# Half of the gate tiles through Gelu straight from PSUM, and a new order of all engines, in a two-layer attention and feed-forward kernel

## The chip, the cores and the metric

The kernel runs on one core of one Trainium2 chip. A core has five engines that run side by side, each through its own queue in order: TensorE (matrix products, PE in the profile), VectorE (DVE), ScalarE (ACT), GpSimd (POOL) and SyncE (SP, which here only issues DMA transfers). TensorE writes into PSUM, and VectorE and ScalarE read from there. The metric is the device time of one execution in microseconds (us).

## The reference

Two blocks A and B are applied in turn, A, B, A, B, to x of 2048 x 512 in bfloat16. A is attention with a compressive memory, over 4 segments of 512 rows, with 32 heads of 16; B is a gated feed-forward layer of inner width 1792.

```python
def A(x, wq, wk, wv, wo, beta):              # x is already layer-normed
    q, k, v = heads(x @ wq), heads(x @ wk), heads(x @ wv)      # 32 heads, 4 segments of 512
    phi = lambda t: where(t > 0, t + 1.0, exp(t))
    g = sigmoid(beta)
    M, z = 0, 0
    for s in range(4):
        p = softmax(q[s] @ k[s].T * 16 ** -0.5 + causal_mask)
        a_dot = p @ v[s]
        a_mem = (phi(q[s]) @ M) / (phi(q[s]) @ z + 1e-6)
        out[s] = g * a_mem + (1 - g) * a_dot
        M += phi(k[s]).T @ v[s];  z += phi(k[s]).sum(0)
    return out @ wo

def B(x, w_gate, w_up, w_down):
    return gelu_tanh(x @ w_gate) * (x @ w_up) @ w_down

x = x + A(layernorm(x));  x = x + B(layernorm(x))      # and both once more
```

## The kernel before, in words

The work falls into eight pieces, numbered k = 0 to 7: segment k % 4 of the first pass (k below 4) or of the second. Each piece has an attention part (class `Att`) and a feed-forward part (class `Ffn`), 512 rows each. Activations, x and all weights stay in SBUF. Almost all matrix products go through `product`, which issues four matmuls of 32 columns each, side by side on the array (profile line L392).

**Scores and exponentials.** A piece has 20 score steps, five for each group of eight heads. A step fills two PSUM tiles `st0` and `st1` (two banks each) by small matmuls (L786); ScalarE takes the exponential of each from PSUM to SBUF (L815, 128x1024, 320 in all); GpSimd clears what the causal mask hides (L806). After two or three steps a "flush" multiplies the result with v (L834). Since there is one `st0` and one `st1`, a score has to wait for the exponential that reads the same tile.

**Everything else** is an item: q, k and v products (`qk`, `v`), memory products (`mem`, `upd`), the output product `wo`, `gate`, `up`, `down`, and for three of the norms a transpose on TensorE (`turn`; the other transposes are DMAs, L357). Every item takes one of four PSUM banks `m0` to `m3`, until VectorE or ScalarE has read it out. `evict` posts such a copy to both engines, and the one that is free first takes it (L383 on VectorE, L384 on ScalarE).

**The order is planned when the program is built.** A small model (`Clocks`, `Engine`) keeps a clock for each engine with fixed costs, and emits the instructions in the order in which the model would run them. On the chip each queue then runs in that fixed order, and waits where the data is not there. At each turn the planner issues a score step if its PSUM tile is free; else the ready item with the lowest due date (`Item.due`, for example `k + 0.61` for `wo`, `k + 1.2` for `gate`); and if there is no ready item, a dummy product on the tile `warm`, whose result nobody reads:

```python
            if streams:
                ps = Psum()
                ...
                product(ps()[:], warm[:], wide)
```

ScalarE's and VectorE's jobs are served by ready time plus a slack (`EXP_SLACK`, `GELU_SLACK`, ...), the lowest first.

**Gelu.** ScalarE needs one function table for the exponentials and another for Gelu; a job with the other table puts a load ahead of it. Each `Ffn` has 14 gate tiles. For k = 0 to 6 they are copied from PSUM to the tile `gel`; when all 14 are there, `gelu_all` posts Gelu over `gel` in place, in groups of `GELU_TILES = 4` tiles (L986: three of 128x2048 and one of 128x1024), with no exponential between. For k = 7 each tile goes from PSUM through Gelu directly (L927), since no exponentials are left. VectorE multiplies `gel` by the up product (L953), then come the four down products.

Of the kernel before, what the change touches and what calls it, by code (L numbers as in the profile page):

```python
# [38 lines left out]
M_BANKS = 4  # L39
PT_STEPS = 5  # L40
SETS = 3
GELU_TILES = 4
QK_DUE = 0.75
E_Q = 0.0
E_K = 0.9

FLUSH_WAIT = 4.0
PIECE_SLACK = 2.0
URGENT, SOON, NORMAL = -4.0, -1.5, 0.0
EXP_SLACK, E_SLACK, PHI_SLACK, GELU_SLACK = -1.0, 3.0, 3.0, -1.0  # L50
ACT_EVICT, FIRST_EVICT = 0.5, 1.0
XN_BUFS = 3
KB_DVE = 1
KB_SLACK = 4.0
HALF_STEPS = 1
MARGIN = 1.0
MEM_SLACK = 1.0


class Engine:  # L60
# [2 lines left out]
    LATENCY = 0.055  # L63

    def __init__(self, overlap=0.0):
        self.free, self.overlap, self.jobs, self.table = 0.0, overlap, [], "exp"

    def post(self, ready, slack, *steps, table=None, taken=None):

# [14 lines left out]
    def serve(self, now):  # L84

        self.jobs = [j for j in self.jobs if not j[4]]
        if not self.jobs:
            return False
        start = max(self.free, min(j[0] for j in self.jobs) + self.LATENCY)
        if start > now:  # L90
            return False
        job = min((j for j in self.jobs if j[0] + self.LATENCY <= start + 0.03), key=lambda j: j[0] + j[1])
        ready, _, steps, table, taken = job
        taken.append(1)
        self.jobs.remove(job)
        t = ready
        if table and table != self.table:
            self.free += 1.28
            self.table = table
        for cost, emit, told in steps:  # L100
            t = max(self.free, t + self.LATENCY) + cost
            self.free = t - self.overlap
            if emit:
                emit()
            if told:
                told(t)
        return True


class Clocks:  # L110


    MM = {512: 0.2158, 128: 0.056}
    SMALL = 0.025
    SWITCH = 0.097

    def __init__(self):
# [100 lines left out]
def kernel(  # L218
# [278 lines left out]
    class Att:  # L497
        def __init__(self, k):
            self.k, self.s, self.tt0 = k, k % NSEG, TPS * (k % NSEG)
            self.norm = Norm(("xnTa", k), self.tt0, f"xnTa{k % 2}", NORMAL, lambda: k < 2 or ("qkv", k - 2) in ev)  # L500
# [9 lines left out]
        def add_items(self):  # L510
            k, s = self.k, self.s

            def storage():
                return k < SETS or (("scores", k - SETS) in ev and self.phi_done(k - SETS))
# [8 lines left out]
            def qk(b, w, done):  # L523
                ps = Psum()
                pairs = [(lambda kt=kt: w[:, kt, b * P:(b + 1) * P], lambda kt=kt: self.norm.xnT[:, kt, :])
                         for kt in range(KT)]
                return Item(k - QK_DUE + 0.01 * b, lambda: storage() and ck.has(("xnTa", k)), dense(ps, pairs),
                            lambda: (made(), self.counted(), done(b, ps)), kind="qk", ps=ps)

            def q_done(b, ps):  # L530
# [28 lines left out]
            def v(j):  # L559
                ps = Psum()  # L560
                pairs = [(lambda kt=kt: self.norm.xnT[:, kt, j * P:(j + 1) * P], lambda kt=kt: w_att["v"][:, kt, :])
                         for kt in range(KT)]

                def done():
                    self.counted()
                    evict(ps, lambda: by_head(self.vaug)[:, j, :, 0:DH],
                          lambda: ps()[:].rearrange("p (h e) -> p h e", e=DH),
                          lambda t: ev.update({("v", k, j): t}))

                return Item(k - QK_DUE + 0.04 + 0.01 * j if k else -0.61,  # L570
                            lambda: ck.has(("xnTa", k)) and (k < SETS or ("flush", k - SETS, 3, 1) in ev),
                            dense(ps, pairs), done, kind="v", ps=ps)

# [50 lines left out]
        def mem_items(self):  # L624
# [10 lines left out]
            def den_done():  # L635
                def add():
# [7 lines left out]
            items.append(Item(k + 0.01, lambda: ready() and (self.s == 1 or ("am", k - 1) in ev),  # L644
                              [(Clocks.SMALL, lambda j=j, b=b: den_mm(j, b)) for j in range(TPS) for b in range(4)],
                              den_done, kind="mem", ps=den))

# [43 lines left out]
        def upd_item(self):  # L691
# [13 lines left out]
            def done():  # L705
# [23 lines left out]
                else:  # L729
# [162 lines left out]
    class Ffn:  # L892
        def __init__(self, k):
            self.k, self.tt0, self.last = k, TPS * (k % NSEG), k >= NSEG
            self.norm = Norm(("xnTf", k), self.tt0, "xnTf", URGENT, lambda: k == 0 or ("up", k - 1) in ev)
            self.n_wo, self.n_gate, self.n_kept, self.n_up, self.n_down = 0, 0, 0, 0, 0

            def add_to_x(j, ps, slack, told):
                xt = x_sb[:, self.tt0 + j, :]
# [3 lines left out]
            def wo(j):  # L903
                ps = Psum()
                pairs = [(lambda kt=kt: att[k].aT[:, kt, j * P:(j + 1) * P], lambda kt=kt: w_att["o"][:, kt, :])
                         for kt in range(KT)]

                def done():
                    add_to_x(j, ps, URGENT, lambda t: self.norm.stats(j, t))
                    self.n_wo += 1  # L910
                    if self.n_wo == TPS:
                        ev["wo", k] = ck.pe

                return Item(k + 0.61 + 0.001 * j, lambda: ck.has(*[("aT", k, b) for b in range(4)]),
                            dense(ps, pairs), done, kind="wo", ps=ps)

            def gate(ft):
                ps = Psum()
                pairs = [(lambda kt=kt: wg_sb[:, kt, ft * P:(ft + 1) * P], lambda kt=kt: self.norm.xnT[:, kt, :])
                         for kt in range(KT)]  # L920

                def done():
# [3 lines left out]
                    if k == NK - 1:  # L926
                        ck.act.post(ck.made(), URGENT, (0.602, lambda: nc.scalar.activation(  # L927
                            out=self.gel[:, ft, :], in_=ps()[:], func=ACT.Gelu_apprx_tanh),
                            lambda t: (ps.read(t), ev.update({("gel", k, ft): t}))), table="gelu")
                        return  # L930

                    def told(t):
                        self.n_kept += 1
                        if self.n_kept == FT:
                            self.gelu_all(t)

                    evict(ps, lambda: self.gel[:, ft, :], lambda: ps()[:], told)

                return Item(k + 1.2 + 0.005 * ft,
                            lambda: ck.has(("xnTf", k)) and (k == 0 or ("down", k - 1) in ev),  # L940
                            dense(ps, pairs), done, kind="gate", ps=ps)

            def up(ft):
# [4 lines left out]
                def done():  # L948
                    self.n_up += 1
                    if self.n_up == FT:  # L950
# [6 lines left out]
                return Item(k + 1.3 + 0.02 * ft, lambda: ck.has(("gel", k, ft), by=ck.pe + 0.6), dense(ps, pairs), done,  # L957
                            kind="up", ps=ps)

            def down(j):  # L960
# [22 lines left out]
        def gelu_all(self, ready):  # L983
            def gelu(f0, f1):
                g = self.gel[:, f0:f1, :]
                return (0.205 + 0.427 * (f1 - f0), lambda: nc.scalar.activation(out=g, in_=g, func=ACT.Gelu_apprx_tanh),  # L986
                        lambda t: ev.update({("gel", self.k, ft): t for ft in range(f0, f1)}))

            ck.act.post(ready, GELU_SLACK, *[gelu(f, min(f + GELU_TILES, FT)) for f in range(0, FT, GELU_TILES)],
                        table="gelu")  # L990

    mem_state = {}
    st_free = [0.0, 0.0]
# [64 lines left out]
    def norm_of_input(s, at, gap):  # L1058
        for j in range(TPS):
# [1 line left out]

    norm_of_input(1, 11.7, 0.5)
    norm_of_input(2, 22.0, 1.0)
    ck.when(lambda: ("v", 1, 3) in ev and all(("k", 1, b) in ev for b in range(4)),
            lambda: norm_of_input(3, ck.pe, 2.0))


    streams = [(k, t) for k in range(NK) for t in range(STEPS)]
# [15 lines left out]
    def score_now(idle=False):  # L1084
        if not streams or not (step_free or half):
            return ()
        k, t = streams[0]
        if not att[k].score_ready(t):
            return ()
        free = [f <= ck.pe - 0.05 for f in st_free]  # L1090
        if half:
            return (1,) if free[1] else ()
        if all(free):
            return (0, 1)
        other = any(not j[4] and j[0] <= st_free[1] for j in ck.act.jobs)
        return (0,) if free[0] and (idle or k < HALF_STEPS and not other) else ()

    def open_item(got):
        it = min(got, key=lambda it: it.due)
# [86 lines left out]
```

## Time and profile before

| | |
|---|---|
| time, median of 3 runs | 565.4 us (564.77 to 566.05) |
| time of the profiled execution | 564.99 us |
| its span, first to last instruction | 563.2 us |
| TensorE matmul busy | 553.9 us (98%) |
| VectorE busy | 464.7 us (83%) |
| ScalarE busy | 446.8 us (79%) |
| GpSimd busy | 273.1 us (48%) |
| granted TensorE clock | 1.000 |

The span is what the trace shows; the time is 1.8 us longer. A group of instructions is a line, an engine, an operation, the tiles out<-in, the shape, xcount, then the busy time and the mean length of one in ns, then the idle time of the engine just before them and what ended it. Neighbouring instructions of an engine overlap a little, so a busy time can be below the count times the mean.

### The profile page before, as it was taken

What the parts mean: (1) busy time and instruction counts of PE and PEld (TensorE: products, weight loads), DVE (VectorE), ACT (ScalarE), POOL (GpSimd) and SP (SyncE); (2) the same over time, 40 slices, a digit from 0 to 9 for tenths busy, and PEclk for the clock granted to TensorE, in tenths of its full rate; (3) what the DMA queues carried; (4) which work ended last, traced back from release to release, by engine and by line L of the source; (5) the groups of instructions that cost most, each with busy time, mean ns of one, the idle gap of its engine ahead of it and who ended that gap; (6) DMA issues with size and microseconds to landing.
All of it is one profiled execution on the core that took longest, in us unless ns stands there. A gap on an engine that the chain in (4) does not pass through costs nothing.

```text
span 563.2 us, 24630 instructions
## 1 busy us (share of the span) xinstructions
PE 553.9 (98%) x10998; PEld 259.7 (46%) x10998; DVE 464.7 (83%) x881; ACT 446.8 (79%) x510; POOL 273.1 (48%) x520
## 2 busy tenths in 40 slices
PE   8999999999999999999999999999999999999997
PEld 4433445444445444444445444444444444445554
DVE  5977999999988899888978999889789976778061
ACT  3899999987899879997889878988799778970600
POOL 2589865465542459336553456535654354410000
PEclk9999999999999999999999999999999999999999
DMA  7236812801130016100210224002320004100001
GB/s 224 40 96 201 148 12 41 171 3 30 32 59 3 12 26 92 31 2 2 43 38 3 31 49 70 10 4 34 77 45 3 3 21 78 21 2 30 12 3 40
DMA packets 64362, 25.98 MB, mean 46 GB/s; under 512 B 54272, under 2 KB 64256, under 8 KB 64256
## 3 DMA queue, kind: packets, MB, share of 16 engines
q1 hardware_dynamic: 64112, 24.40, 21.4%
q8 instruction: 86, 1.41, 1.1%
q14 instruction: 20, 0.16, 0.1%
q10 hardware_dynamic: 144, 0.01, 0.0%
HBM read 9.71 MB, written 2.10 MB: 21 GB/s over the span
## 4 chain that ended last, share of the span: by engine, by line
PE 82%; DVE 15%; issue 1%; DMA 1%; POOL 0%; ACT 0%; DVEq 0%
PE m L392 66%; PE st L786 8%; PE m L834 5%; DVE st L415 2%; DVE x_sb L900 2%; DVE byq L846 1%; PE m L297 1%; DVE e L604 1%; DVE phiq L604 1%; DVE e L618 1%; DVE xn L445 1%; DVE aT L861 1%; DVE gel L383 1%; DMA amT<-am 1%; DVE ab L854 1%
## 5 line engine op out<-in xcount | busy, mean ns | idle before, releaser
L815 ACT ACTIVATE pt<-st 128x1024 bf16<-128x1024 f32 x320 | 310.4, 1027 | 56.4 <-PE st L786 52.6
L806 POOL TENSOR_SCALAR_AFFINE_SELECT pt<-pt 128x256 bf16<-128x256 bf16 (+1 forms) x448 | 205.6, 478 | 203.9 <-ACT pt L815 197.6
L392 PE MATMUL m<-xnT,wg_sb 128*32 128x512 bf16 x1792 | 107.9, 380 | 1.3 <-ACT xnT L384 0.7
L392 PE MATMUL m<-wd_sb,gel 128*32 128x512 bf16 x1792 | 105.3, 380 | 0.1
L392 PE MATMUL m<-xnT,wu_sb 128*32 128x512 bf16 x1792 | 104.1, 379 | 0.0
L953 DVE TENSOR_TENSOR gel<-gel,m 128x512 bf16<-128x512 bf16 x112 | 75.1, 684 | 26.9 <-PE m L392 25.5
L392 PEld LDWEIGHTS <-wu_sb 128*32 128x32 bf16 x1792 | 46.8, 97 | 46.6 <-issue 4.4
L392 PEld LDWEIGHTS <-gel 128*32 128x32 bf16 x1792 | 46.0, 97 | 46.0 <-issue 6.2
L392 PEld LDWEIGHTS <-wg_sb 128*32 128x32 bf16 x1792 | 45.5, 96 | 46.0 <-issue 10.3
L900 DVE TENSOR_TENSOR x_sb<-x_sb,m 128x512 bf16<-128x512 bf16 x64 | 42.5, 675 | 22.0 <-PE m L392 21.6
L846 DVE STREAM_TRANSPOSE byq<-m 128x512 f32<-128x512 f32 x64 | 45.0, 705 | 11.9 <-PE m L834 11.8
L543 POOL TENSOR_SCALAR kB<-kf,maskB 128x512 bf16<-128x512 bf16 x28 | 45.0, 1609 | 18.9 <-DVE kf L383 13.0
L383 DVE CAST gel<-m 128x512 bf16<-128x512 f32 x56 | 37.9, 683 | 10.7 <-PE m L392 10.3
L834 PE MATMUL m<-pt,vaug 128*32 128x512 bf16 (+3 forms) x1024 | 46.2, 300 | 0.1
L986 ACT ACTIVATE gel<-gel 128x2048 bf16<-128x2048 bf16 (+1 forms) x28 | 45.2, 1685 | 0.1
L415 DVE BATCH_NORM_STATS2 st<-x_sb 128x6 f32<-128x512 bf16 x60 | 40.6, 676 | 0.3
L786 PE MATMUL st<-q,kB 32*128 32x128 bf16 (+3 forms) x512 | 39.8, 300 | 1.0 <-ACT pt L815 0.9
L786 PE MATMUL st<-q,kf 16*128 16x128 bf16 (+3 forms) x512 | 39.5, 302 | 0.7 <-ACT pt L815 0.7
L834 PEld LDWEIGHTS <-vaug 128*32 128x32 bf16 x1024 | 25.6, 97 | 22.1 <-issue 2.1
L392 PE MATMUL m<-xnT,wq_sb 128*32 128x512 bf16 x496 | 34.5, 381 | 0.0
L392 PE MATMUL m<-xnT,wk_sb 128*32 128x512 bf16 x496 | 33.9, 380 | 0.0
L392 PE MATMUL m<-wv_sb,xnT 128*32 128x512 bf16 x512 | 32.3, 380 | 0.0
(93 smaller groups left out, 568.7 us busy)
## 6 DMA issues: line engine op xcount, KB each, us to landing
out_dram<-x_sb SPq DMA_DIRECT2D x16, 128.0 KB, 1.8
wg_sb<-in_B_w_gate_dram SPq DMA_DIRECT2D x8, 224.0 KB, 5.2
wu_sb<-in_B_w_up_dram SPq DMA_DIRECT2D x8, 224.0 KB, 3.7
wd_sb<-in_B_w_down_dram SPq DMA_DIRECT2D x7, 256.0 KB, 3.7
x_sb<-in_A_x_dram SPq DMA_DIRECT2D x3, 512.0 KB, 6.2
xnT<-xn SPq DMA_TRANSPOSE x48, 2.5
x_sb<-in_A_x_dram SPq DMA_DIRECT2D x4, 128.0 KB, 3.1
wv_sb<-in_A_wv_dram SPq DMA_DIRECT2D x1, 512.0 KB, 7.1
```

The lines of the kernel that those rows point to most:

```text
L383: ck.dve.post(ck.made(), slack, (0.673, lambda: nc.vector.tensor_copy(out=dst(), in_=src()), end), taken=taken)
L392: nc.tensor.matmul(out[r], lhsT=lhsT[:, r], rhs=rhs, start=start, stop=stop, tile_position=(0, 32 * c))
L415: nc.vector.bn_stats(out=self.st6[:, 0, :], in_=x_sb[:, self.tt0 + j, :])
L543: job.post(t, KB_SLACK if k else NORMAL, (cost, lambda: eng.tensor_scalar(out=self.kB[:, b, :], in0=self.kf[:, b, :], scalar1=maskB[:, 0:1 ...
L786: nc.tensor.matmul(sts[j // 2][:, j % 2, c0:c0 + N], lhsT=lhsT[rows, b, P * ki:P * ki + P], rhs=self.q[rows, b, P * ki:L], start=True, sto ...
L806: nc.gpsimd.affine_select(out=dv, in_=dv, pattern=[[0, w], [1, P]], compare_op=ALU.is_ge, fill=0.0, base=0, channel_multiplier=-1)
L815: ck.act.post(max(begun + 0.4, self.step_from), EXP_SLACK, (1.024, lambda st=st, pt=pt: nc.scalar.activation(out=pt[:], in_=st[:], func=AC ...
L834: nc.tensor.matmul(ps()[32 * j:32 * j + 32, P * ki:L], lhsT=self.vaug[:, ki, h * (DH + 1):h * (DH + 1) + 32], rhs=two[j // 2][:, j % 2, c0 ...
L846: nc.vector.transpose(out=self.byq[:, par, :, :].rearrange("p a c -> p (a c)"), in_=ps()[:])
L900: ck.dve.post(ck.made(), slack, (0.683, lambda: nc.vector.tensor_tensor(out=xt, in0=xt, in1=ps()[:], op=ALU.add), lambda t: (ps.read(t), t ...
L953: ck.dve.post(ck.made(), NORMAL, (0.683, lambda: nc.vector.tensor_tensor(out=g, in0=g, in1=ps()[:], op=ALU.mult), lambda t: (ps.read(t), e ...
L986: return (0.205 + 0.427 * (f1 - f0), lambda: nc.scalar.activation(out=g, in_=g, func=ACT.Gelu_apprx_tanh), lambda t: ev.update({("gel", se ...
```

## The change

For k = 0 to 6 the first seven gate tiles (`RAW = 7`) are copied to `gel` as before, and Gelu is posted for them in groups of `GELU_TILES = 2` once the seven are there (three pairs and a single one). The other seven go from PSUM through Gelu directly. From the first of these on, ScalarE's planner is told to hold back exponentials (`hold`), until all 14 tiles are done. The gate items have to come in the order of their tiles, and those behind the eighth are given a due date that puts them ahead of nearly all else. For k = 7 all 14 go directly, as before. Due dates, slacks and one cost (`SMALL`) get new values, with a correction for each kind and piece (`DUE`, `DUE_STEP`, `BIAS`). `HALF_FROM = 0`, `XT = 2` and `N3 = 0.0` keep the old behaviour.

```diff
-GELU_TILES = 4
-QK_DUE = 0.75
-E_Q = 0.0
-E_K = 0.9
+GELU_TILES = 2
+RAW = 7
+QK_DUE = 0.628
+E_Q = -0.224
+E_K = 0.898
...
-EXP_SLACK, E_SLACK, PHI_SLACK, GELU_SLACK = -1.0, 3.0, 3.0, -1.0
-ACT_EVICT, FIRST_EVICT = 0.5, 1.0
+EXP_SLACK, E_SLACK, PHI_SLACK, GELU_SLACK = -0.824, 4.309, 2.973, 1.704
+ACT_EVICT, FIRST_EVICT = 1.257, 1.549
...
+DUE = {"wo": 0.876, "gate": 1.264, "up": 1.3, "down": 1.912, "upd": 0.119, "mem": 0.057, "v": -0.028}
+DUE_STEP = {"gate": 0.0055, "up": 0.02, "down": 0.0585}
+BIAS = {
+    **{("qk", k): d for k, d in {2: 0.223, 3: 0.042, 4: 0.068, 5: 0.154, 6: 0.166, 7: 0.076}.items()},
...
     def serve(self, now):
         self.jobs = [j for j in self.jobs if not j[4]]
-        if not self.jobs:
+        able = [j for j in self.jobs if not self.hold or j[3] != "exp"]
+        if not able:
             return False
-        start = max(self.free, min(j[0] for j in self.jobs) + self.LATENCY)
+        start = max(self.free, min(j[0] for j in able) + self.LATENCY)
...
-    SMALL = 0.025
+    SMALL = 0.033
...
-            items.append(Item(k + 0.45, ready, [(Clocks.MM[128], lambda c=c: m(c)) for c in range(n_mm)],
+            items.append(Item(k + DUE["upd"] + BIAS.get(("upd", k), 0), ready, [(Clocks.MM[128], lambda c=c: m(c)) for c in range(n_mm)],
...
+                    if ft < raw:
+                        def kept(t):
+                            self.kept.append(t)
+                            if len(self.kept) == raw:
+                                for f0 in range(0, raw, GELU_TILES):
+                                    f1 = min(f0 + GELU_TILES, raw)
+                                    r = slice(f0, f1)
+                                    ck.act.post(max(self.kept), GELU_SLACK, (
+                                        0.205 + 0.427 * (f1 - f0), gelu(lambda r=r: g[:, r, :], lambda r=r: g[:, r, :]),
+                                        lambda t2, r=r: told(t2, range(r.start, r.stop))), table="gelu")
+
+                        evict(ps, lambda: g[:, ft, :], lambda: ps()[:], kept)
+                    else:
+                        if k < NK - 1:
+                            ck.act.hold = True
+                        ck.act.post(ck.made(), URGENT, (0.602, gelu(lambda: g[:, ft, :], lambda: ps()[:]),
+                                                        lambda t: (ps.read(t), told(t, [ft]))), table="gelu")
-                return Item(k + 1.2 + 0.005 * ft,
-                            lambda: ck.has(("xnTf", k)) and (k == 0 or ("down", k - 1) in ev),
+                return Item((-2.0 if ft > RAW else k) + DUE["gate"] + BIAS.get(("gate", k), 0) + DUE_STEP["gate"] * ft,
+                            lambda: ck.has(("xnTf", k)) and (k == 0 or ("down", k - 1) in ev) and self.n_gate == ft,
                             dense(ps, pairs), done, kind="gate", ps=ps)
...
-                return Item(k + 1.6 + 0.05 * j, lambda: ck.has(*[("h", k, ft) for ft in range(FT)]),
+                return Item(k + DUE["down"] + BIAS.get(("down", k), 0) + DUE_STEP["down"] * j, lambda: ck.has(*[("h", k, ft) for ft in range(FT)]),
                             dense(ps, pairs), done, kind="down", ps=ps)
...
-        def gelu_all(self, ready):
...
```

More of the change, by code (lines that the diff above doesn't have):

```diff
@@ L65, in __init__ @@
     def __init__(self, overlap=0.0):
-        self.free, self.overlap, self.jobs, self.table = 0.0, overlap, [], "exp"
+        self.free, self.overlap, self.jobs, self.table, self.hold = 0.0, overlap, [], "exp", False
     def post(self, ready, slack, *steps, table=None, taken=None):
@@ L86, in serve @@
         self.jobs = [j for j in self.jobs if not j[4]]
-        if not self.jobs:
+        able = [j for j in self.jobs if not self.hold or j[3] != "exp"]
+        if not able:
             return False
-        start = max(self.free, min(j[0] for j in self.jobs) + self.LATENCY)
+        start = max(self.free, min(j[0] for j in able) + self.LATENCY)
         if start > now:
             return False
-        job = min((j for j in self.jobs if j[0] + self.LATENCY <= start + 0.03), key=lambda j: j[0] + j[1])
+        job = min((j for j in able if j[0] + self.LATENCY <= start + 0.03), key=lambda j: j[0] + j[1])
         ready, _, steps, table, taken = job
@@ L526, in qk @@
                          for kt in range(KT)]
-                return Item(k - QK_DUE + 0.01 * b, lambda: storage() and ck.has(("xnTa", k)), dense(ps, pairs),
+                return Item(k - QK_DUE + BIAS.get(("qk", k), 0) + 0.01 * b, lambda: storage() and ck.has(("xnTa", k)), dense(ps, pairs),
                             lambda: (made(), self.counted(), done(b, ps)), kind="qk", ps=ps)
@@ L568, in done @@
                           lambda t: ev.update({("v", k, j): t}))
-                return Item(k - QK_DUE + 0.04 + 0.01 * j if k else -0.61,
+                return Item(k - QK_DUE + BIAS.get(("v", k), 0) + DUE["v"] + 0.01 * j if k else -0.61,
                             lambda: ck.has(("xnTa", k)) and (k < SETS or ("flush", k - SETS, 3, 1) in ev),
@@ L642, in den_done @@
                              lambda t: ev.update({("den", k): t})))
-            items.append(Item(k + 0.01, lambda: ready() and (self.s == 1 or ("am", k - 1) in ev),
+            items.append(Item(k + DUE["mem"] + BIAS.get(("mem", k), 0), lambda: ready() and (self.s == 1 or ("am", k - 1) in ev),
                               [(Clocks.SMALL, lambda j=j, b=b: den_mm(j, b)) for j in range(TPS) for b in range(4)],
@@ L912, in done @@
                         ev["wo", k] = ck.pe
-                return Item(k + 0.61 + 0.001 * j, lambda: ck.has(*[("aT", k, b) for b in range(4)]),
+                return Item(k + DUE["wo"] + BIAS.get(("wo", k), 0) + 0.001 * j, lambda: ck.has(*[("aT", k, b) for b in range(4)]),
                             dense(ps, pairs), done, kind="wo", ps=ps)
@@ L920, in gate, with gelu, told @@
                          for kt in range(KT)]
+                def gelu(out, in_):
+                    return lambda: nc.scalar.activation(out=out(), in_=in_(), func=ACT.Gelu_apprx_tanh)
+                def told(t, tiles):
+                    for f in tiles:
+                        ev["gel", k, f] = t
+                    self.n_gel += len(tiles)
+                    if self.n_gel == FT:
+                        ck.act.hold = False
                 def done():
@@ L925, in done @@
                     self.n_gate += 1
[L926 to L937, printed above, removed]
-                return Item(k + 1.2 + 0.005 * ft,
-                            lambda: ck.has(("xnTf", k)) and (k == 0 or ("down", k - 1) in ev),
+                    g = self.gel
+                    raw = RAW if k < NK - 1 else 0
+                    if ft < raw:
[16 more added lines that the diff above has]
+                            lambda: ck.has(("xnTf", k)) and (k == 0 or ("down", k - 1) in ev) and self.n_gate == ft,
                             dense(ps, pairs), done, kind="gate", ps=ps)
@@ L955, in done @@
                         lambda t: (ps.read(t), ev.update({("h", k, ft): t}))))
-                return Item(k + 1.3 + 0.02 * ft, lambda: ck.has(("gel", k, ft), by=ck.pe + 0.6), dense(ps, pairs), done,
+                return Item(k + DUE["up"] + BIAS.get(("up", k), 0) + DUE_STEP["up"] * ft, lambda: ck.has(("gel", k, ft), by=ck.pe + 0.6), dense(ps, pairs), done,
                             kind="up", ps=ps)
@@ L981, in __init__ @@
                          + [up(ft) for ft in range(FT)] + [down(j) for j in range(TPS)])
-        def gelu_all(self, ready):
[L984 to L990, printed above, removed]
     mem_state = {}
@@ L1063 @@
     norm_of_input(2, 22.0, 1.0)
-    ck.when(lambda: ("v", 1, 3) in ev and all(("k", 1, b) in ev for b in range(4)),
-            lambda: norm_of_input(3, ck.pe, 2.0))
+    if N3:
+        norm_of_input(3, N3, 1.0)
+    else:
+        ck.when(lambda: ("v", 1, 3) in ev and all(("k", 1, b) in ev for b in range(4)),
+                lambda: norm_of_input(3, ck.pe, 2.0))
     streams = [(k, t) for k in range(NK) for t in range(STEPS)]
@@ L1095, in score_now @@
         other = any(not j[4] and j[0] <= st_free[1] for j in ck.act.jobs)
-        return (0,) if free[0] and (idle or k < HALF_STEPS and not other) else ()
+        return (0,) if free[0] and (idle and k >= HALF_FROM or k < HALF_STEPS and not other) else ()
     def open_item(got):
```

26 lines of the change are left out of this document (19 added, 7 removed).

## The prediction

> **What bounds the kernel now.** I read the page first (shares, slices, the chain that ended last). "..." marks lines that are left out.
>
> ```profile
> span 563.2 us, 24630 instructions
> ...
> PE 553.9 (98%) x10998; PEld 259.7 (46%) x10998; DVE 464.7 (83%) x881; ACT 446.8 (79%) x510; POOL 273.1 (48%) x520
> ...
> PEclk9999999999999999999999999999999999999999
> ...
> PE 82%; DVE 15%; issue 1%; DMA 1%; POOL 0%; ACT 0%; DVEq 0%
> ```
>
> TensorE is busy for 553.9 of 563.2 us, at a clock that never drops, and makes 82% of the chain that ended last. ScalarE and VectorE have some 100 us to spare each. So two things can shorten the run: fewer TensorE instructions, or less of the 9.3 us in which TensorE stands still. Next: how much of TensorE's work is not needed? The planner issues a dummy product on `warm` whenever nothing else is ready. The view of one tile's instructions by stretch, for `warm`, and one piece of the chain give the amount and the price:
>
> ```profile
> 12.00:92.00 80.00, 7.56 (x104) 2.33 (x104) 0.00 (x0) 1.00 0.41 91
> 92.00:487.00 395.00, 1.02 (x12) 0.25 (x12) 0.00 (x0) 1.00 0.21 37
> 487.00:563.20 76.20, 3.09 (x44) 0.99 (x44) 0.00 (x0) 1.00 0.05 16
> ...
> 523.44 36.47 PE m L392 x672
> ```
>
> The second column is TensorE's busy time and, in brackets, its matmuls. A product is four matmuls side by side on the array, so 160 dummy matmuls are 40 products: 26 in the opening, 3 later, 11 just before the last exponentials. The chain row is an undisturbed piece: 672 matmuls, 168 products, in 36.47 us, 0.217 us a product. The dummies thus take 40 x 0.217 = 8.7 us of the span.
>
> Then I asked which engine makes TensorE idle, or use dummies, and where (windows; columns: stretch, length, busy us and count of PE, PEld, DVE, ACT, POOL, then clock, DMA share, GB/s):
>
> ```profile
> 0.00:20.00 20.00, 18.12 (x176) 7.77 (x176) 13.04 (x39) 11.01 (x17) 7.88 (x23) 1.00 0.51 159
> ...
> 520.00:563.20 43.20, 39.19 (x736) 21.77 (x728) 13.16 (x20) 9.92 (x16) 0.00 (x0) 1.00 0.06 21
> sum 563.20, PE 553.92 PEld 259.73 DVE 464.67 ACT 446.78 POOL 273.09; mean PE 36.93 PEld 17.32 DVE 30.98 ACT 29.79 POOL 18.21
> ...
> 12.00:92.00 80.00, 79.18 (x1504) 33.70 (x1506) 72.13 (x155) 75.97 (x96) 59.82 (x107) 1.00 0.41 91
> ```
>
> Of the 9.28 us idle, 1.88 fall in the first 20 us and 4.01 in the last stretch, which the change hardly touches; 3.4 us are spread between. In the opening (12 to 92 us) ScalarE is busy 75.97 of 80 us: there the exponentials set the pace, and the dummies fill TensorE's wait for them. From then on TensorE is the bound.
>
> **The change part by part.** *Dummies.* In the built order of the changed kernel 44 dummy matmuls are left, 11 products, all ahead of the 51st exponential; the matrix work is otherwise the same, instruction for instruction. Gone are 29 x 0.217 = 6.3 us. That this is on the path follows from the bound: behind the opening TensorE's own queue sets the end, and work done early is work not done late. In the new order the products done before the 65th exponential include 16 more of v and 3 more of gate (and 17 small ones of the memory fewer); the 11 dummies ahead of the last exponentials vanish because the last Gelu group now stands ahead of 8 exponentials instead of 4, with other products to run beside it. **-6.3 us.**
>
> *Mode changes.* TensorE goes between score tiles and dense products 364 times instead of 360. The price of one, from the timeline of TensorE:
>
> ```profile
> 300.85 4.49 PE L392 MATMUL m<-xnT,wu_sb 128*32 128x512 bf16 x80
> 305.28 0.29 PE L786 MATMUL st<-q,kf 16*128 16x256 bf16 x4
> ```
>
> 80 matmuls are 20 products, 4.34 us, and the score starts 4.43 after the first: 0.1 us. Four make **+0.4 us**.
>
> *Opening on ScalarE.* Up to the 64th exponential the new order gives ScalarE 28 evictions instead of 25, and 10 small exponentials (`e`) instead of 11. ScalarE's timeline prices them by the start of what follows:
>
> ```profile
> 58.31 0.67 ACT L600 ACTIVATE e<-kf 128x512 bf16<-128x512 bf16 x1
> 58.84 1.98 ACT L815 ACTIVATE pt<-st 128x1024 bf16<-128x1024 f32 x2
> ...
> 63.52 1.11 ACT L384 ACTIVATE vaug<-m 128x512 bf16<-128x512 f32 x2
> 64.50 1.95 ACT L815 ACTIVATE pt<-st 128x1024 bf16<-128x1024 f32 x2
> ```
>
> An eviction holds the queue for 0.49 us, a small exponential for 0.53: 3 x 0.49 - 0.53 = 0.9 us more in a stage that ScalarE sets. The cover is ScalarE's idle 4.0 of 80 us there. Bounds 0 (all in the idle time) and 0.9; I take the middle, **+0.4 us**.
>
> *Gelu.* Per layer half (seven of eight; the last keeps its form) seven tiles are no longer copied and then turned in groups of four, but go from PSUM through Gelu. The groups of instructions:
>
> ```profile
> L986 ACT ACTIVATE gel<-gel 128x2048 bf16<-128x2048 bf16 x21 | 38.6, 1900 | 0.1
> L384 ACT ACTIVATE gel<-m 128x512 bf16<-128x512 f32 x42 | 24.7, 611 | 0.5 <-PE m L392 0.3
> L986 ACT ACT_TABLE_LOAD x7 | 9.0, 1283 | 0.1
> L815 ACT ACT_TABLE_LOAD x7 | 9.0, 1283 | 0.1
> L927 ACT ACTIVATE gel<-m 128x512 bf16<-128x512 f32 x14 | 8.0, 599 | 2.5 <-PE m L392 2.4
> L986 ACT ACTIVATE gel<-gel 128x1024 bf16<-128x1024 bf16 x7 | 7.3, 1041 | 0.0
> L383 DVE CAST gel<-m 128x512 bf16<-128x512 f32 x56 | 37.9, 683 | 10.7 <-PE m L392 10.3
> ```
>
> 98 copies of gate tiles become 49 (24 on VectorE instead of 56, 25 on ScalarE instead of 42). Of the q, kf, vaug and xnT copies the new order moves 11 from VectorE to ScalarE. VectorE thus loses 32 + 11 = 43 copies, 43 x 0.68 = 29 us of 464.7. ScalarE: -17 x 0.61 + 49 x 0.60 - (38.6 + 7.3) + 21 x 1.04 + 7 x 0.6 + 11 x 0.61 = +6 us, on an engine that is 79% busy. Neither is on the path as a total. The table loads stay 16.
>
> What counts is the stretch in which exponentials are held, for the scores behind them wait for PSUM. In the middle of the kernel before, ScalarE's timeline shows one:
>
> ```profile
> 291.82 1.94 ACT L815 ACTIVATE pt<-st 128x1024 bf16<-128x1024 f32 x2 [0.64 <-PE st L786]
> 293.77 1.28 ACT L986 ACT_TABLE_LOAD   x1
> 295.07 6.46 ACT L986 ACTIVATE gel<-gel 128x2048 bf16<-128x2048 bf16 x4
> 301.55 1.28 ACT L815 ACT_TABLE_LOAD   x1
> 302.84 1.94 ACT L815 ACTIVATE pt<-st 128x1024 bf16<-128x1024 f32 x2
> ```
>
> From 293.77 to 302.84 no exponential runs, 9.07 us. TensorE meanwhile has dense products, and the first score that has to wait for these exponentials starts at 305.28 (the row above), 0.5 us after the exponential that frees its PSUM (302.84 + 1.94): hidden, with 0.5 us to spare. The new stretch: two loads 2.57, three pairs 3.12, one single 0.60, seven direct ones 4.19, less the overlap of neighbours (6.46 for the four against 6.74 added up: 0.09 each of ten) 0.9: 9.6 us, 0.5 us longer. That uses the spare time up. In the new order TensorE has gate and up products in each stretch, about as many as before. If it stays covered it costs 0; if the 0.5 us shows in all seven, 3.5. The nearest row is the spare 0.5 us, so I take little: **+0.3 us**. Queued behind a direct Gelu are the rest of the Gelus, the load back and the exponentials; a direct one also holds one of the four PSUM banks until ScalarE comes.
>
> *Relief.* With VectorE 29 us emptier, evictions that are late today may come in time. That can't give more than the 3.4 us idle in the middle. I take 0.
>
> *DMA queue.* The SyncE queue keeps its transfers, only interleaved anew; the down weights stay behind about the same transposes. 0.
>
> Sum against the profiled execution, 564.99 us (1.8 us around its span of 563.2; 0.4 below the median of 565.4): 564.99 - 6.3 + 0.4 + 0.4 + 0.3 = 564.99 - 5.2 = **559.8 us**.
>
> **The rivals.** *Relief* (12%): the idle 3.4 us go as well: 556.4. For: VectorE loses 29 us. Against: where TensorE waits, ScalarE is named more than VectorE, in the groups with the most idle time (last columns):
>
> ```profile
> L392 PE MATMUL m<-xnT,wg_sb 128*32 128x512 bf16 x1792 | 107.9, 380 | 1.3 <-ACT xnT L384 0.7 <-DVE am L661 0.3 <-DVE gel L383 0.3
> ...
> L786 PE MATMUL st<-q,kB 32*128 32x128 bf16 (+3 forms) x512 | 39.8, 300 | 1.0 <-ACT pt L815 0.9
> L786 PE MATMUL st<-q,kf 16*128 16x128 bf16 (+3 forms) x512 | 39.5, 302 | 0.7 <-ACT pt L815 0.7
> ```
>
>
> *The opening gives it back* (18%): ScalarE is the bound there, so the 15 dummies that go from it become waits, 15 x 0.217 = 3.3 us: 563.1. For: 75.97 busy of 80. Against: the new order places real products in their room.
>
> *The hold overflows* (10%, the slower side): TensorE fills its four banks with gates while ScalarE loads the table, and each stretch comes out longer than its cover by one table load, 1.28 us: 7 x 1.28 = 9.0, 568.8. It decides from 5.2 / 7 = 0.74 us of stall a stretch. For: the spare time is 0.5 us. Against: gates take 4 x 0.217 = 0.87 us each, longer than the 0.60 us of a direct Gelu, so ScalarE catches up.
>
> *The clock falls* (2%). The dummies also keep the array busy. The view of the tile `warm` (min/median/max ns) and the chain:
>
> ```profile
> L392 PE MATMUL m<-warm x160: 376/379/390, 24.2 to 492.6; 128*32 128x512 bf16 x160
> L297 PE MATMUL m<-warm x22: 379/620/634, 1.1 to 10.7; 128*128 128x512 bf16 x22
> ...
> 1.11 6.97 PE m L297 x19
> ```
>
> The first matmuls of the kernel take 620 ns, later ones 379. Were one long stall of 3 us to bring that slow stretch back, it costs 3 + 19 x 0.24 = 7.6 us: 567.4. Against: between 20 and 520 us only 3.4 us idle in all. The Trainium skill (TensorE: Matmul & The Clock Gate, Part 1) says that the array falls to half clock after an idle window of about 3.4 us, and needs such a window of work to come back; the trace agrees with the slow start, and shows no fall later. By that rule dummies may go as long as no single wait nears it, and the sum stays as it is.
>
> That the change doesn't do what it says is excluded by the built order: 49 direct Gelus, 16 table loads, 11 dummies.
>
> **How the numbers follow.** The forecast of 559.8 (its own span 558 to 561.5) has 58%. The range: at the low end relief, 556.4; at the high end forecast with the upper bounds of opening and stretches, 559.8 + 0.5 + 3.2 = 563.5, which also takes in the opening's rival; about 2 in 10 stay outside. A difference of 0.2%, 1.1 us, is what can be told from no change. Faster by more: forecast 58, relief 12, most of the opening 15: 85%. Within: 5% (opening and a hold that costs about what the dummies gave). Slower: 10%, the hold and the clock.
>
> **What would show it.** Right: 44 dummy matmuls in the profile after, TensorE busy near 548, ScalarE near 453, VectorE near 436 us; the loads 16; TensorE's idle time still near 9 us. Opening wrong: the score tiles wait on ScalarE for clearly more than the 1.6 us of the two rows above, in the first 90 us. Hold wrong: in stretches between table loads, TensorE's scores or gates wait on ScalarE for over 0.7 us each. Relief: idle under 7 us. The prediction is wrong if TensorE's idle time grows by as much as its busy time falls.

## The result, and the profile after

The kernel after takes 558.03 us (median of 4, 557.85 to 559.25) against 565.09 us before; the ratio is 0.9875, 95% interval 0.9863 to 0.9887. That is 1.25% faster, 7.1 us. The prediction was 559.8 us, with 556.4 to 563.5 as its range. The profiled execution of the kernel after took 559.25 us, the slowest of the four, and is 5.7 us under the profiled one of before.

The page of the kernel after, lines as in the prediction:

```profile
span 557.5 us, 24388 instructions
...
PE 547.4 (98%) x10882; PEld 255.0 (46%) x10882; DVE 436.5 (78%) x838; ACT 446.8 (80%) x553; POOL 270.4 (48%) x520
...
PEclk9999999999999999999999999999999999999999
...
PE 83%; DVE 10%; ACT 2%; DMA 1%; issue 1%; POOL 1%; SPq 0%; ACTq 0%
```

TensorE lost 6.5 us of busy time and 116 matmuls, which are the 29 dummy products, and its idle time stayed about the same: 557.5 - 547.4 = 10.1 us, where it was 9.3. VectorE lost 28 us; TensorE's idle time shows no gain from it. By stretch (columns as before: stretch, length, busy us and count of PE, PEld, DVE, ACT, POOL, clock, DMA share, GB/s):

```profile
12.00:92.00 80.00, 79.77 (x1498) 32.97 (x1500) 72.43 (x155) 78.27 (x99) 61.29 (x107) 1.00 0.37 90
```

In the opening ScalarE is even fuller (78.27 of 80 us; 75.97 before), and TensorE waits less (0.23 us; 0.82). The view of the tile `warm` by stretch shows the dummies that are left:

```profile
12.00:92.00 80.00, 3.46 (x44) 0.80 (x44) 0.00 (x0) 1.00 0.37 90
92.00:487.00 395.00, 0.00 (x0) 0.00 (x0) 0.00 (x0) 1.00 0.20 37
```

The stretch in which exponentials are held, on ScalarE's timeline near the middle of the kernel:

```profile
283.90 1.28 ACT L943 ACT_TABLE_LOAD   x1
285.20 1.08 ACT L943 ACTIVATE gel<-m 128x512 bf16<-128x512 f32 x2
286.17 1.06 ACT L943 ACTIVATE gel<-gel 128x1024 bf16<-128x1024 bf16 x1
...
290.44 1.62 ACT L943 ACTIVATE gel<-gel 128x1024 bf16<-128x1024 bf16 x2
292.08 1.28 ACT L834 ACT_TABLE_LOAD   x1
293.38 1.94 ACT L834 ACTIVATE pt<-st 128x1024 bf16<-128x1024 f32 x2
```

It lasts from 283.90 to 293.38, 9.5 us, against 9.07 before. Who TensorE waited for in all (waits of PE):

```profile
PE m L411 <- DMA phik<-e: 1.7, 1, 1.7
PE st L805 <- ACT pt L834: 1.3, 3, 0.6
```

Scores wait for exponentials three times in the whole kernel, 1.3 us. The one long wait is of another kind: a DMA transpose of `phik` (phi(k), which the memory's update reads) lands late.

### The profile page after: what moved, and what is told of

Its sections match the earlier page's. It is cut to its first block, busy times and chain, and to the rows that moved or that the text cites. A ratio compares the mean times of both kernels' runs of the same rounds, so it can differ in the third digit from the quotient of the medians.

```text
span 557.5 us, 24388 instructions
## 1 busy us (share of the span) xinstructions
PE 547.4 (98%) x10882; PEld 255.0 (46%) x10882; DVE 436.5 (78%) x838; ACT 446.8 (80%) x553; POOL 270.4 (48%) x520
## 4 chain that ended last, share of the span: by engine, by line
PE 83%; DVE 10%; ACT 2%; DMA 1%; issue 1%; POOL 1%; SPq 0%; ACTq 0%
PE m L411 68%; PE st L805 9%; PE m L853 6%; ACT pt L834 1%; DVE x_sb L920 1%; DVE byq L865 1%; DVE xn L464 1%; DVE e L623 1%; DVE gel L990 1%; ACT gel L943 1%; DMA phik<-e 1%; DVE e L637 1%; DVE phiq L623 1%; DMA x_sb<-in_A_x_dram 1%; DVE aT L880 1%
## 5 line engine op out<-in xcount | busy, mean ns | idle before, releaser
L825 POOL TENSOR_SCALAR_AFFINE_SELECT pt<-pt 128x256 bf16<-128x256 bf16 (+1 forms) x448 | 202.6, 471 | 218.0 <-ACT pt L834 212.4
L990 DVE TENSOR_TENSOR gel<-gel,m 128x512 bf16<-128x512 bf16 x112 | 75.3, 684 | 44.2 <-PE m L411 34.8
L411 PE MATMUL m<-xnT,wg_sb 128*32 128x512 bf16 x1792 | 106.6, 380 | 0.7 <-ACT xnT L403 0.7
L411 PE MATMUL m<-wd_sb,gel 128*32 128x512 bf16 x1792 | 106.8, 380 | 0.1
L411 PE MATMUL m<-xnT,wu_sb 128*32 128x512 bf16 x1792 | 105.8, 380 | 0.1
L805 PE MATMUL st<-q,kB 32*128 32x384 bf16 (+3 forms) x512 | 39.6, 300 | 1.3 <-ACT pt L834 1.3
L805 PE MATMUL st<-q,kf 16*128 16x384 bf16 (+3 forms) x512 | 40.1, 302 | 0.1
L943 ACT ACTIVATE gel<-m 128x512 bf16<-128x512 f32 x63 | 34.8, 602 | 3.7 <-PE m L411 3.5
L411 PE MATMUL m<-xnT,wk_sb 128*32 128x512 bf16 x496 | 35.4, 381 | 0.0
L411 PE MATMUL m<-wv_sb,xnT 128*32 128x512 bf16 x512 | 33.9, 380 | 0.0
L805 PEld LDWEIGHTS <-kf 16*128 16x128 bf16 x512 | 11.9, 91 | 43.7 <-issue 42.2
```

What stands on the lines that cost most here:

```text
L411: nc.tensor.matmul(out[r], lhsT=lhsT[:, r], rhs=rhs, start=start, stop=stop, tile_position=(0, 32 * c))
L805: nc.tensor.matmul(sts[j // 2][:, j % 2, c0:c0 + N], lhsT=lhsT[rows, b, P * ki:P * ki + P], rhs=self.q[rows, b, P * ki:L], start=True, sto ...
L825: nc.gpsimd.affine_select(out=dv, in_=dv, pattern=[[0, w], [1, P]], compare_op=ALU.is_ge, fill=0.0, base=0, channel_multiplier=-1)
L943: return lambda: nc.scalar.activation(out=out(), in_=in_(), func=ACT.Gelu_apprx_tanh)
L990: ck.dve.post(ck.made(), NORMAL, (0.683, lambda: nc.vector.tensor_tensor(out=g, in0=g, in1=ps()[:], op=ALU.mult), lambda t: (ps.read(t), e ...
```

## The experiments

Two theories stood at first. **A**: a dummy product is work in TensorE's queue, and the kernel is faster because 29 of them are gone. **B**: a dummy stands in a wait that would be there without it, and the kernel is faster because real products stand in these places now.

### Dummies not issued

In both kernels the order stays and only the dummy product is left out (its result is not read by anything):

```diff
-                product(ps()[:], warm[:], wide)
+                ck.tiling("columns")
                 ck.on_pe(Clocks.MM[512])
```

Before, without its 40 dummies:

> The kernel before, with the same planned order on every engine; only its 40 dummy products are not issued (the planner still counts their time). Theory A (a dummy is work on the path, and the changed kernel is faster because 29 of them are gone): 40 x 0.217 = 8.7 us less, plus about 12 mode changes fewer at 0.1, so about 555.5 us, faster than the changed kernel's 558.0, and TensorE's idle time stays near 9 us. Theory B (a dummy stands where TensorE would wait for ScalarE or VectorE anyway; the changed kernel is faster because it has real products in these places): the time stays near 565 us (564 to 566), and TensorE's idle time grows by some 9 us, most of it before 92 us and around 485 us.

Measured: 567.59 us against 564.92 (ratio 1.0040, interval 1.0024 to 1.0055): slower, not 8.7 us faster. Its windows:

```profile
12.00:92.00 80.00, 74.43 (x1378) 31.21 (x1380) 70.58 (x153) 75.01 (x94) 58.44 (x106) 0.96 0.38 92
...
25.36:28.77 3.41, 1.85 (x32) 0.77 (x32) 3.31 (x8) 3.34 (x4) 1.24 (x3) 1.00 0.57 89
28.77:32.18 3.41, 3.41 (x30) 0.70 (x24) 2.67 (x6) 2.37 (x3) 3.06 (x7) 0.50 0.51 176
73.14:76.55 3.41, 1.89 (x44) 0.86 (x47) 3.34 (x9) 3.41 (x5) 2.27 (x5) 1.00 0.24 38
76.55:79.96 3.41, 3.22 (x68) 1.71 (x60) 3.31 (x8) 3.13 (x5) 1.32 (x4) 0.50 0.02 5
```

TensorE is idle where the dummies stood, 5.6 us in the opening instead of 0.8, and ScalarE works no faster for it. On top of that the granted clock falls to 0.50 twice, for 3.41 us each time, right after 3.41 us with 1.5 to 1.6 us of idle time. TensorE's timeline shows how short the single waits ahead of the second fall were:

```profile
74.20 0.39 PE L786 MATMUL st<-q,kf 16*128 16x384 bf16 x4 [1.17 <-ACT pt L815]
...
78.40 1.81 PE L392 MATMUL m<-xnT,wq_sb 128*32 128x512 bf16 x16
```

The longest single wait there is 1.17 us, and ahead of the first fall 0.52 us; yet the 16 matmuls (4 products) at 78.40 take 1.81 us instead of the 1.05 us that 16 such matmuls show elsewhere. Two such stretches cost at most 3.4 us together. By this estimate the slower time is the clock's; without the falls the profiled execution, 566.45 us, would be at most some 2 us under the kernel before, not 8.7. Theory A falls.

After, without its 11:

> The changed kernel in its own planned order, without issuing its 11 dummy products. Theory A: 11 x 0.217 = 2.4 us less, about 555.6 us. Theory B: no change, 557.5 to 558.5 us, and 2 us more idle time of TensorE before 75 us. Apart from that: if the wait of 1.9 us on a transposed phik near 404 us in the profile of the changed kernel belongs to the kernel, it shows here again; if it is a chance delay of one execution, it is gone.

Measured: 557.94 us (557.03 to 559.81), the same as the 558.03 with dummies, and TensorE idles 1.6 us in the opening instead of 0.2. This agrees with B, but the four executions spread over 2.8 us, more than the 2.4 us in question, so the run alone decides little. In the profiled execution (557.42 us) the wait on phik was gone.

### Product time added behind the opening

```diff
...
+                    ops[0] = (cost, lambda: (product(ps()[:], warm[:], wide), first()))      # ops of each down item, k < 7
```

> The changed kernel with its order unchanged on all engines, and one dummy product more at the head of each of the 28 down items of the first seven pieces (28 x 0.217 = 6.1 us of TensorE work, nearly all of it behind the opening, into the PSUM bank that the item owns anyway, so no wait is added). Theory B': behind the opening TensorE's queue is the bound, so product time there is paid in full, and the kernel gained because the new order does 16 more real products in the opening, in slots that were dummies: 558.0 + 6.1 = 564 us. Rival: TensorE has hidden slack there too (other waits set the pace): less than 3 us more, below 561 us.

Measured: 563.26 us, 5.2 us over the kernel after (4.2 us between the profiled executions); 28 products are 6.1 us. Some 70 to 85% of added product time is paid, so behind the opening TensorE's queue is mostly the bound. A real product that moves from there into a slot of the opening can be worth most of its time; a dummy that was only dropped gave nothing in either kernel.

### Fewer dummies in other plans

Only the due dates of q, k and v, in the kernel before:

```diff
-QK_DUE = 0.75
+QK_DUE = 0.628          # and the new corrections of the q, k and v items
```

> The kernel before with nothing but the due dates of the q, k and v items changed to those of the changed kernel (Gelu as before, all other dates and slacks as before). Planned anew it has 15 dummy products instead of 40; ahead of the 64th exponential 13 instead of 26, with 16 products of v more and the small memory products later. If the filling of the opening is the source of the gain: the 200th exponential starts 4 to 6 us earlier than before (313.8 us), and the kernel takes 565.1 - 25 x 0.217 = 559.7 us, unless waits come up later as in the other plans: 558 to 562 us. If the gain needs the direct Gelus: the 200th exponential at 312 us or later and 563 us or more.

Measured: 565.12 us, ratio 0.9998 (0.9989 to 1.0007): no change, with 25 dummies fewer. The 201st exponential (the one that the expectation means by its 313.8) starts at 312.8 us. By these numbers the expectation's second case holds, but further below the other new dates and slacks prove enough for the early scores without direct Gelus. Windows of this kernel, and then of the kernel before for the second stretch:

```profile
92.00:107.00 15.00, 12.83 (x280) 6.39 (x271) 13.84 (x27) 14.88 (x15) 5.99 (x9) 1.00 0.70 135
138.00:158.00 20.00, 18.09 (x464) 9.19 (x460) 18.19 (x38) 19.47 (x26) 13.67 (x25) 1.00 0.35 49
```

```profile
138.00:158.00 20.00, 19.27 (x478) 8.88 (x471) 19.11 (x40) 17.91 (x23) 12.43 (x25) 1.00 0.22 45
```

TensorE idles 2.2 us in the first stretch and 1.9 in the second (before 0.7): the slots came back as waits. In the first TensorE waits mostly for two copies on VectorE (kf 1.25 us, q 0.77), in the second mostly for exponentials (0.51, 0.40 and 0.24 us). That ScalarE and VectorE were full (14.88 and 13.84 of 15 us in the first) does not explain it alone: in the kernel before they were as full from 92 to 107 us, with TensorE idle for 0.5 us.

The new Gelu with all the old dates:

```diff
-DUE = {"wo": 0.876, "gate": 1.264, ...
+DUE = {"wo": 0.61, "gate": 1.2, ...          # BIAS empty, slacks and SMALL as before
...
```

> The changed kernel's Gelu (seven tiles copied, seven directly, exponentials held), with the due dates, slacks and the cost SMALL of the kernel before; planned anew, it holds 29 dummy products (before 40, changed 11). If the Gelu path makes the gain, it lies near 558 us. If the gain follows the dummies whatever makes them fewer: 565.1 - 11 x 0.217 = 562.7 us. If direct Gelus cost more in the held stretches than they give: 565 us or more.

Measured: 575.87 us, 11 us slower than before. The opening keeps its 26 dummies, and the 201st exponential starts at 313.5 us, as before (313.8). Most of the loss comes late; one piece, from TensorE's timeline and a window:

```profile
524.61 3.19 PE L402 MATMUL m<-wd_sb,gel 128*32 128x512 bf16 x56
529.99 1.05 PE L402 MATMUL m<-ident,xn 128*32 128x128 bf16 x48 [2.19 <-DVE xn L455]
531.84 0.41 PE L402 MATMUL m<-ident,xn 128*32 128x128 bf16 x16 [0.80 <-DVE xn L455]
533.05 13.74 PE L402 MATMUL m<-xnT,wg_sb 128*32 128x512 bf16 x224 [0.80 <-DVE xnT L393]
```

```profile
527.00:538.00 11.00, 7.22 (x148) 3.23 (x144) 4.32 (x11) 4.27 (x6) 1.26 (x2) 0.84 0.04 13
```

Only one down item (3.2 us) is left to cover the last norm, so TensorE waits 2.19, 0.80 and 0.80 us, and the clock falls (a mean of 0.84 over these 11 us). In the kernel after, the same norm has three down items beside it. By its number the expectation's third case holds, but no run separates what the direct Gelus cost here from what the old dates cost with them.

The new dates with the old Gelu, and the same with 1 us more counted for the transposed phik of one piece:

```diff
-GELU_TILES = 2
-RAW = 7
+GELU_TILES = 4
+RAW = 14
...
+                                ck.act.hold = True
```

> The new due dates and slacks, with all 14 gate tiles copied and turned in groups of four (exponentials held meanwhile, so no table load is added); planned anew, it holds 18 dummy products. If the gain follows the dummies: 565.1 - 22 x 0.217 = 560.3 us. If the direct Gelus are what makes the gain: about 564 to 565 us.

> The new dates with the old Gelu (14 tiles copied, groups of four) as in the earlier run at 567.6 us, but the planner counts 1 us more until a transposed phik of piece 5 has landed, so that its update is planned later; 12 dummy products. If that run lost by waits of TensorE on the transposed phik near 406 us (3.1 us there) and by what follows them: about as fast as the changed kernel, 557 to 561 us, and the direct Gelus are worth less than 2 us. If direct Gelus are needed: 564 us or more.

Measured: 567.60 and 562.71 us, 0.4% slower and 0.4% faster than the kernel before; neither is where its expectation had it. Both have the new opening (11 dummies ahead of the 51st exponential), and their 201st exponential starts at 308.0 and 307.7 us, against 309.6 in the kernel after. So the new dates alone bring the score stream forward by 6 us up to there, and the direct Gelus add nothing to it. Windows from 92 to 314 us show where the plans part (before, after, q, k and v dates alone, new dates with old Gelu):

```profile
92.00:314.00 222.00, 220.22 (x4480) 102.72 (x4476) 199.41 (x374) 195.08 (x217) 113.25 (x214) 1.00 0.20 37
92.00:314.00 222.00, 220.11 (x4504) 102.41 (x4496) 182.62 (x348) 196.83 (x242) 112.78 (x217) 1.00 0.20 38
92.00:314.00 222.00, 217.82 (x4456) 102.39 (x4447) 195.44 (x366) 196.22 (x220) 114.68 (x214) 1.00 0.21 38
92.00:314.00 222.00, 219.52 (x4464) 102.18 (x4456) 195.65 (x365) 199.26 (x222) 111.75 (x219) 1.00 0.19 37
```

With the q, k and v dates alone TensorE idles 4.2 us here, in the others 1.8 to 2.5. From the start to 314 us its idle time and its dummies (0.217 us each) add up to 10.1 us before, 6.5 after, 9.6 with the q, k and v dates alone and 7.0 with all new dates and the old Gelu. So the real products in the opening pay only in a plan that brings no new waits behind it, and the other new dates and slacks, not the direct Gelus, see to that. Which of them do it is not shown.

Then the plans with the old Gelu lose it. In the first:

```profile
406.36 0.30 PE L411 MATMUL m<-vaug,phik 128*32 128x128 bf16 x8
408.44 0.24 PE L411 MATMUL m<-vaug,phik 128*32 128x128 bf16 x4 [1.77 <-DMA phik<-e]
409.72 0.73 PE L411 MATMUL m<-vaug,phik 128*32 128x128 bf16 x36 [1.04 <-DMA phik<-e]
```

These are waits of 2.8 us on transposed phik. The margin brought 4 to 5 us back, but not the 557 to 561 us expected: waits of 1.28 and 0.38 us on phik stayed at the same place, followed by 3.41 us at half clock. What of the remaining 4.7 us against the kernel after belongs to the direct Gelus is not separated.

Another split, nine tiles copied and five direct (`RAW = 9`):

> The changed kernel with nine tiles copied first and five taken directly, planned anew with the same due dates, 11 dummies as well. If the gain comes from the dates' order and not from the exact split, it stays within 1% of the changed kernel: 555 to 562 us. If the dates fit only the split of seven that they were chosen with, as the old dates with the new Gelu did (575.9), it loses most of the gain: 563 us or more.

Measured: 568.13 us, slower than before, with 11 dummies. The 201st exponential is early again (307.5 us), and the loss comes later: 1.9 us on phik near 406, and the waits of 2.18, 0.80 and 0.80 us on the last norm, as in the new Gelu with old dates.

### The hold

```diff
-                            ck.act.hold = True
+                            pass
```

> The changed kernel without holding exponentials back while direct Gelus are due; planned anew, ScalarE gets 42 table loads instead of 16 and TensorE 36 dummy products instead of 11. If ScalarE's table loads can hide in its idle time (20% of the span): near the changed kernel plus the dummies, 558 + 0 to 5 us. If each load of 1.28 us stalls the scores: 26 x 1.28 = 33 us at most; with ScalarE idle for about 100 us I expect about a third of it: some 570 us.

Measured: 585.94 us, 28 us over the kernel after; my third of 33 us was too small. Its groups of table loads:

```profile
L943 ACT ACT_TABLE_LOAD x21 | 26.9, 1283 | 3.9 <-PE m L411 3.5
L834 ACT ACT_TABLE_LOAD x20 | 25.7, 1283 | 0.4
```

The 26 loads added are 33 us of ScalarE, and the kernel is longer by 84% of that, although ScalarE is idle for a fifth of the span on average. The new order also has 25 dummies more, so how much of the 28 us is the loads alone is not separated.

### The wait on phik

Stores planned behind the transposes, and 2.5 us more counted until phik of piece 5 has landed:

```diff
-                        ck.sp.post(t, URGENT, (0.5, lambda: load(of[...
+                        ck.sp.post(t, 20.0, (0.5, lambda: load(of[...
```

> The changed kernel, with the stores of finished rows put behind the DMA transposes that are due on the same queue (slack 20 instead of URGENT); planned anew, still 11 dummies. Theory: the wait of 1.9 us on a transposed phik near 404 us comes from a store of 128 KB issued just ahead of it, so it vanishes here: 0 to 2 us less than 558.0, 556 to 557.5, and no execution near 559. Rival: the transposes themselves are slow at times (2.5 us against 1.2 to issue), whatever stands ahead: no change, 558 us, and the wait shows up at another place.

> The changed kernel with 2.5 us more counted until a transposed phik of piece 5 has landed; order unchanged up to there, 11 dummies. If the wait near 404 us (1.9 us in the profile of the changed kernel) is what separates its slower from its faster executions: 0 to 2 us less than 558.0, that is 556 to 558 us, with no execution above 558.5. If the new order behind it has waits of its own: 558 us or more.

Measured: 562.20 and 558.66 us; neither is faster than the kernel after, and the first is 4 us slower, which neither theory expected. In the first, TensorE's timeline and a window:

```profile
402.01 0.35 PE L411 MATMUL m<-vaug,phik 128*32 128x128 bf16 x12
404.75 1.04 PE L411 MATMUL m<-vaug,phik 128*32 128x128 bf16 x48 [2.38 <-DMA phik<-e]
```

```profile
402.00:409.00 7.00, 4.62 (x104) 2.24 (x100) 3.01 (x7) 3.24 (x4) 2.91 (x6) 0.76 0.45 112
```

With no store ahead of the transposes the wait is longer, since this plan puts the update earlier; the store is not its cause. Behind the wait the clock halves for 3.41 us, which makes the mean of 0.76 over the window shown. The transposes landed 2.4 to 4.1 us after issue in the kernel after, and these plans have the update 1.4 to 2.4 us behind the issue of the last of them. In the second, the wait came again (1.65 us). Why the landing varies stays open.

## Why the prediction was right, and where it was not

**The dummies, -6.3 us.** The size holds, but not the simple reading. Exactly the 44 dummy matmuls that the built order showed are left. What counts is the sum of TensorE's idle time (span less busy) and its dummies (0.217 us each), in the profiled executions:

| kernel | dummies | their us | idle us | sum | median us |
|---|---|---|---|---|---|
| before | 40 | 8.7 | 9.3 | 18.0 | 565.1 |
| before, dummies not issued | 0 | 0 | 16.8 | 16.8 | 567.6 |
| before, q, k, v dates | 15 | 3.3 | 13.6 | 16.9 | 565.1 |
| new Gelu, old dates | 29 | 6.3 | 17.9 | 24.2 | 575.9 |
| old Gelu, new dates | 18 | 3.9 | 14.0 | 17.9 | 567.6 |
| the same with the margin | 12 | 2.6 | 12.3 | 14.9 | 562.7 |
| after, nine copied | 11 | 2.4 | 16.6 | 19.0 | 568.1 |
| after | 11 | 2.4 | 10.1 | 12.5 | 558.0 |
| after, dummies not issued | 0 | 0 | 9.2 | 9.2 | 557.9 |

Between before and after this sum fell by 5.5 us, and the profiled time by 5.7. The sum is bookkeeping: the rest of the span is TensorE's time on real products, 545.2 us before and 545.0 after, and longer where the clock falls (550 with the new Gelu and the old dates). The prediction carried the idle time in one clause, that it stays near 9 us, and gave no row for it; it did stay (10.1). In six of the seven other rows it did not (12.3 to 17.9 us), and counting dummies alone missed these times by up to 13 us. So that the clause held for this plan is in part luck. The step that was right is the one behind the number: in the opening 16 more products of v stand where dummies stood, and behind it most of the time of a product is paid. It is not enough by itself: the q, k and v dates alone have the same 16 products there, and gained nothing. Of the 5.5 us, 3.6 are there by 314 us, and the new dates with the old Gelu have 3.1 by then; how the rest divides between the dates and the direct Gelus is not shown. The rival "the opening gives it back" fell: the row 12 to 92 shows less idle time, not more.

**Mode changes (+0.4) and opening (+0.4).** The first can't be told apart. The second cost nothing that shows: ScalarE took the additional work out of its idle time there (4.0 us before, 1.7 after).

**The Gelu stretch (+0.3).** Predicted 9.6 us, measured 9.5 in the stretch shown; scores wait for exponentials 1.3 us in all, as little as before. The overflow rival fell. But the direct Gelus earned no part of the gain up to the 201st exponential, and without the hold the price is 28 us.

**Engine totals.** VectorE 436.5 us, predicted near 436. ScalarE 446.8, predicted near 453: I added means, though neighbours overlap by about 0.1 us, and the kernel after has 43 more instructions on ScalarE (63 direct Gelus of 0.602 us are busy for 34.8 us, not 37.9).

**The clock.** No fall in the kernel after, as predicted. But what I drew from the rule in the Trainium skill (TensorE: Matmul & The Clock Gate, Part 1), that dummies may go as long as no single wait nears 3.4 us, disagrees with the runs: with single waits of at most 0.52 and 1.17 us ahead of it the clock fell to half, and the kernel without dummies was slower. The measurement decides: in the opening of the kernel before, dummies keep the clock up, and cost some 2 us at most. A fall also costs less than the 7.6 us of the prediction: 3.41 us at half clock are at most 1.7 us.

**The remainder.** Against the profiled executions the forecast (-5.2) missed by 0.5 us. The median is 1.2 us lower still; a wait of 1.7 us on phik is in the profiled execution, and was absent from the profiled one without dummies.

## What to carry to other kernels

Where a planner fills waits with dummy work, count dummies and idle time of the bounding engine together; a dummy that was only removed gave nothing here, and one that is replaced by real work from a bound stretch can give most of its time, as long as the plan does not give the slot back as a wait. A fixed order is fitted to all its parts at once: each half of this change alone, and a split of nine instead of seven, was slower than before, and with 1 us more counted for one transpose the half with the new dates was 0.4% faster. So a part's worth can't be read from the whole, and a plan with fewer dummies still has to be measured.

## What the hardware showed that I had not expected

TensorE's granted clock falls without any long idle time. In these traces it is 1.00 or 0.50, and a fall lasts 3.41 us (once 6.83); a value such as 0.83 over 10 us is a mean over such a stretch. The 3.41 us ahead of a fall held 1.5 to 1.6 us of idle time in single waits of at most 0.52 and 1.17 us in the kernel before without its dummies, 1.7 us in the new dates with the old Gelu and the margin, and 2.4 us in the kernel with late stores. But 3.41 us with 1.7 us idle (404.47 to 407.88) passed at full clock in the kernel after, and in the kernel without the hold a fall followed on 0.74 us. So neither the longest wait nor the idle time settles it; what does stays open. Three DMA transposes of 128x512 in one piece landed 2.4, 3.9 and 4.1 us after issue in one execution of the kernel after.
